# Small routing operations on GpSimd, and weight splits 2 to 4 queued behind the last tiles' routing

## The chip, the cores and the metric

The kernel runs on one core of a Trainium2 chip. The metric is the device time of one launch in microseconds (us). A core has five engines that run side by side, each with its own queue in a fixed order: TensorE (PE in the profile, its weight loads PEld), VectorE (DVE), ScalarE (ACT), GpSimd (POOL) and SyncE (SP), which here only issues transfers.

## The reference, cut to what matters

```python
def reference(q, k, v, moe, moe2):
    # attention: 2 x 8 heads, 576 rows, head size 64; only the 32 largest scores of a row count
    scores = q @ k.T / 8
    kth = np.partition(scores, -32, axis=-1)[..., -32:-31]
    attn = softmax(np.where(scores >= kth, scores, -1e9))
    x = heads_side_by_side(attn @ v)                    # 1152 tokens x 512
    # a gated layer, 512 -> 1536 -> 512
    xn = x / np.sqrt(np.mean(x * x, -1) + 1e-6) * rms_g
    x = (silu(xn @ w_gate) * (xn @ w_val)) @ w_out
    # 8 experts, each token goes to one, at most 288 tokens each, in the tokens' order
    e = np.argmax(x @ router, axis=1)
    for each expert: y = np.maximum(x[its tokens] @ w1[e], 0) @ w2[e]
    return y * softmax(x @ router)[e]                   # 1152 x 512
```

## The kernel before

The 1152 tokens are nine tiles of 128 (`t` = 0 to 8). A tile has four **units** of two heads (`p` = 0 to 35). The function `topk` finds the 32 largest scores of a unit on VectorE: for each head four MAX8 (L324, L336) and three MATCH_REPLACE8 (L333) over 128x576 scores. Beside it run, as generators that are advanced a step at a time:

- `scores` (L310 on TensorE, copy L312 on ScalarE) for the next unit. The score tile `s` has four buffers, so the scores of unit p+1 need the two buffers of unit p-1, which are read last in `weights`, by the subtraction L353 on GpSimd. `weights` itself needs the bias that GpSimd makes of `topk`'s results (L326, L338).
- `values` (L376, L377, L384), `norm` (L389 on), `moe1` (the gated layer: TensorE L450 and L475, GpSimd L465, L466, L470), and `dispatch` (the routing of a tile).
- `convert_all`, in the first 220 us or so: it turns the weights of the gated layer, which come as 64-bit words, into pairs of 16-bit values. `bits` (L157 to L160) and `split` (L219 on) do the large work; `gram` and `scale` (L176 to L217) find a scale for each of the seven weight blocks, in operations on one or four columns.

`dispatch(t)` finds each token's expert and place. On VectorE it has the largest logit (L526), a key (L533), the largest key (L536), a one-hot row `oh` (L539), the expert's first row by a product with `first` and a sum (L547), the token's place by the same with a TensorE result (L550), the overflow test (L553), two additions (L554, L563) and the output scale (L555). TensorE counts with `oh` (L542, L543). GpSimd then writes the tile's 128 rows to their slots in `disp` in memory (L565, the **scatter**). Every token must be scattered before an expert's rows can be read back (`gather`, L772), apart from a first group "a" of 128 rows of expert 0, which is read as soon as tile 7 is scattered; it is issued on ScalarE.

After the attention, expert weights are loaded (L718), measured (`size`: squares L731 on ScalarE, then a chain of one-column operations on VectorE) and split into two 16-bit parts (`convert`: L756 on ScalarE, L758 and L761 on VectorE). Weight 4 is loaded into the buffer that weight 2 leaves, weight 5 into that of weight 3. Then `up` and `down` (L845 to L864) run expert by expert, and `send` (L879 on) writes the result.

A scheduler orders the instructions of each engine when the kernel is built, by priorities (`ahead`, L578) and its own model of durations; what it made is fixed in the program. `tc.issue_after(x)` (L814) makes the instructions of its block on the engine of `x` stand behind `x`. In this kernel it stands over `size(3, 3)` and `convert(3, 3)` with a GpSimd instruction, and neither function has one on GpSimd, so it holds nothing back.

## Time and profile before

| what | value |
|---|---|
| three runs | 708.5, 710.47, 710.53 us; median 710.47 us |
| the profiled execution: its own time | 708.96 us |
| its span, first to last instruction | 707.2 us (1.8 us lie around it) |
| VectorE busy | 627.0 us, 89% of the span |
| TensorE busy | 555.5 us, 79% |
| ScalarE busy | 495.8 us, 70% |
| GpSimd busy | 414.9 us, 59% |

Times inside the program are us from the start of the span. Three parts follow each other: attention with the routing of the first tiles beside it, the gated layer and routing of the last tiles, and the experts. A busy share over the whole span mixes them, so it is read for each part. Instructions of one engine overlap a little at their ends, which a sum of durations counts twice.

### The profile page before, as it was taken

How to read it: one execution, taken by the hardware profiler on the slowest of the kernel's cores; microseconds unless marked ns; L12 is line 12 of the kernel's file. 1: busy time of each engine (PE TensorE's matmuls, PEld its weight loads, DVE VectorE, ACT ScalarE, POOL GpSimd, SP SyncE). 2: the span in 40 equal slices, each digit the busy share in tenths (PEclk: the TensorE clock that was granted, in tenths of full speed). 3: DMA queues.
4: the chain of work that ended last, by engine and by line, in shares of the span. 5: the costliest groups of instructions: out<-in, count | busy, mean ns of one | idle time of the engine just before them, and what ended most of it. 6: DMA issues, size and time to landing. Idle time of an engine off the chain costs nothing.

```text
span 707.2 us, 13015 instructions
## 1 busy us (share of the span) xinstructions
PE 555.5 (79%) x4708; PEld 401.9 (57%) x4708; DVE 627.0 (89%) x1311; ACT 495.8 (70%) x959; POOL 414.9 (59%) x444
## 2 busy tenths in 40 slices
PE   1207424567667999999999999998999489989995
PEld 1106324435344666666656666664645289989994
DVE  3999999999999999999999999999348855999960
ACT  3446537558957879868878797876799537988921
POOL 2786887877696887966767778566631110022312
PEclk9999555679999999999999999999999889999998
DMA  8898171375000001000000000000570449999201
GB/s 244 236 331 282 39 233 38 126 225 188 15 8 8 16 31 43 16 31 10 16 23 16 24 16 24 1 1 16 205 286 1 148 82 382 328 322 347 106 21 38
DMA packets 47016, 80.00 MB, mean 113 GB/s; under 512 B 18732, under 2 KB 23340, under 8 KB 46946
## 3 DMA queue, kind: packets, MB, share of 16 engines
q1 hardware_dynamic: 43954, 74.02, 33.2%
q0 software_dynamic: 1792, 4.83, 1.9%
q8 instruction: 39, 0.64, 0.4%
q10 hardware_dynamic: 1200, 0.26, 0.2%
q14 instruction: 31, 0.25, 0.1%
HBM read 64.35 MB, written 12.27 MB: 108 GB/s over the span
## 4 chain that ended last, share of the span: by engine, by line
DVE 49%; issue 16%; PE 11%; ACT 8%; DMA 8%; POOL 6%; SPq 1%; POOLq 0%; ACTq 0%; DVEq 0%
DVE r L333 14%; DVE m L336 14%; DVE m L324 5%; PE pm L450 4%; DMA wbig<-in_w_out_dram 3%; DVE wbig L157 3%; ACT junk L731 3%; DMA raw<-in_w_dram 3%; POOL out_dram L887 2%; DVE wbig L159 2%; DVE split L761 2%; DVE wbig L228 2%; DMA vt<-in_v_l_dram 2%; PE pm L475 2%; DVE hT L423 1%
## 5 line engine op out<-in xcount | busy, mean ns | idle before, releaser
L450 PE MATMUL pm<-wbig,xn 128*128 128x512 f16 x600 | 152.1, 387 | 8.8 <-POOL wbig L225 3.2
L336 DVE MAX8 m<-r 128x8 f32<-128x576 f32 x216 | 156.8, 745 | 0.3
L845 PEld LDWEIGHTS <-split 128*128 128x128 f16 x1728 | 115.6, 99 | 6.9 <-DMA xbT<-xb 2.5
L310 PE MATMUL tp<-kst,qh 128*128 128x288 f32 (+1 forms) x160 | 65.2, 418 | 63.5 <-ACT s L312 24.2
L353 POOL TENSOR_TENSOR pp<-s,pp 128x576 f32<-128x576 f32 x72 | 102.8, 1442 | 8.6 <-ACT pp L352 8.4
L333 DVE MATCH_REPLACE8 r<-m,r 128x576 f32<-128x576 f32 x144 | 106.3, 740 | 0.0
L450 PEld LDWEIGHTS <-xn 128*128 128x128 f16 x648 | 62.4, 100 | 71.9 <-issue 11.3
L475 PE MATMUL pm<-wbig,hT 128*128 128x512 f16 x324 | 79.1, 383 | 7.7 <-POOL wbig L229 3.7
L310 PEld LDWEIGHTS tp<-kst,qh 128*128 128x128 f32 (+1 forms) x160 | 32.6, 205 | 89.9 <-ACT s L312 32.7
L376 PE MATMUL tp<-ident,pp 128*128 128x128 f32 x324 | 58.7, 298 | 16.1 <-ACT pp L358 7.5
L352 ACT ACTIVATE pp<-s,bias 128x576 f32<-128x576 f32 x72 | 52.0, 773 | 26.4 <-POOL bias L338 26.2
L312 ACT ACTIVATE s<-tp 128x288 f32<-128x288 f32 x144 | 54.8, 412 | 19.2 <-POOL pp L353 15.8
L761 DVE SCALAR_TENSOR_TENSOR split<-raw,sc,split 128x2048 f16<-128x2048 f32 (+1 forms) x32 | 65.8, 2078 | 0.1
L887 POOL DMA_INDIRECT out_dram<-ob,tos x14 | 20.2, 1445 | 73.8 <-ACT ob L885 58.4
L845 PE MATMUL acc<-hE,split 128*128 128x168 f16 (+2 forms) x864 | 58.8, 228 | 3.4 <-ACT junk L731 1.4
L731 ACT ACTIVATE junk<-raw 128x2048 bf16<-128x2048 f32 (+1 forms) x32 | 54.2, 1693 | 9.9 <-DMA raw<-in_w_dram 9.5
L384 PE MATMUL xps<-pt,vt 128*64 128x128 f32 (+1 forms) x800 | 57.8, 284 | 2.9 <-ACT pt L377 2.9
L376 PEld LDWEIGHTS tp<-ident,pp 128*128 128x128 f32 x324 | 42.5, 152 | 31.0 <-ACT pp L358 10.3
L377 ACT ACTIVATE pt<-tp 128x384 f32<-128x384 f32 x108 | 49.3, 494 | 14.9 <-PE tp L376 12.3
L845 PE MATMUL acc<-xgT,split 128*128 128x168 f16 (+1 forms) x768 | 58.0, 239 | 0.0
L358 ACT ACTIVATE pp<-pp,bias 128x576 f32<-128x576 f32 x72 | 56.4, 785 | 0.1
L324 DVE MAX8 m<-s 128x8 f32<-128x576 f32 x72 | 53.6, 745 | 0.0
(198 smaller groups left out, 1233.4 us busy)
## 6 DMA issues: line engine op xcount, KB each, us to landing
raw<-in_w_dram SPq DMA_DIRECT2D x28, 1024.0 KB, 10.2
wbig<-in_w_out_dram SPq DMA_DIRECT2D x6, 1024.0 KB, 8.1
disp<-wraw SPq DMA_DIRECT2D x18, 257.0 KB, 5.5
qraw<-in_q_l_dram SPq DMA_DIRECT2D x72, 64.0 KB, 2.2
wraw<-in_w_gate_dram SPq DMA_DIRECT2D x8, 512.0 KB, 4.5
split<-in_w_dram SPq DMA_DIRECT2D x4, 1024.0 KB, 5.8
kraw<-in_k_l_dram SPq DMA_DIRECT2D x12, 288.0 KB, 4.4
wbig<-in_w_val_dram SPq DMA_DIRECT2D x3, 1024.0 KB, 7.4
```

The source lines that it names most:

```text
L310: nc.tensor.matmul(sp[:c1], x[:, i, :c1], kst[b, hp][:, i, c * HALF:(c + 1) * HALF], start=(n == 0), stop=(n == 1))
L324: nc.vector.max(m[:, i, 0], s[i])
L333: nc.vector.match_replace(r[i], m[:, i, n - 1], src, -3.0e38)
L336: nc.vector.max(m[:, i, n], r[i])
L353: nc.gpsimd.tensor_tensor(w, s[i], w, op=OP.subtract)
L376: nc.tensor.transpose(tp[:, i, :], p2[:, o:o + P], ident)
L384: nc.tensor.matmul(xps[t][rows, hp, c0:c1], v, w, start=(n == 0), stop=(n == 4))
L450: nc.tensor.matmul(a, xn[:, x + c, :], half(i, lo), start=(c == 0 and n == 0), stop=(c == KC - 1 and n == 2))
L475: nc.tensor.matmul(yps, hT[f // KC][:, KC * hi + f % KC, :], half(i, lo), start=(f == 0 and n == 0), stop=(f == NF1 - 1 and n == 2))
L731: nc.scalar.activation(junk, raw[:, g * 2 * BIG // k:(g + 1) * 2 * BIG // k], AF.Square, accum_out=sc[:, 9 + g:10 + g])
L761: nc.vector.scalar_tensor_tensor(lo[:, r], raw[:, r], sc[:, 7:8], hi[:, r], op0=OP.mult, op1=OP.subtract)
L845: nc.tensor.matmul(a, u[:, c, col * P:(col + 1) * P], v[:, c, :a.shape[-1]], start=(c == 0 and n == 0), stop=(c == nk - 1 and n == 2))
```

## The change

It has two halves.

**Operations that move from VectorE to GpSimd.** For tiles 0 to 7: `oh` (L539), the overflow test, the first addition and the output scale (L553 to L555), the slot (L563), and the sum of `norm` (L391). The expert's first row comes from the key `k8` by one multiply-add instead of the product with `first`, and the slot is one operation on pos with two scalars. The last tile keeps these on VectorE. In `gram` and `scale` the one- and four-column operations move too (L189, L198, L203 to L208, L212, L213, L215). Counted in the built program, VectorE has 86 instructions fewer and GpSimd 85 more.

**Where splits and squares stand.** `after(t, ...)` places the work of `convert(2, 2)` behind tile 7's routing (its exponential on ScalarE, its reciprocal on VectorE), that of `convert(3, 3)` behind the last tile's (its exponential on ScalarE, its slot on VectorE), and the squares of weight 4 behind the last tile's exponential on ScalarE.

```diff
-    first = const.tile([P, E], F32, name="first")
-    nc.gpsimd.iota(first, pattern=[[cap, E]], base=0, channel_multiplier=0, allow_small_or_imprecise_dtypes=True)
...
             if b < 6:
-                nc.vector.tensor_tensor(m[:, 0:1], m[:, 0:1], g2[:, 0:1], op=OP.mult)
+                nc.gpsimd.tensor_tensor(m[:, 0:1], m[:, 0:1], g2[:, 0:1], op=OP.mult)
...
         def scale(b, g):
             for _ in g:
                 pass
-            v = nc.vector
+            v = nc.gpsimd
...
-                v.tensor_tensor(tmp[:, 0:1], unit[:, 0:1], unit[:, 1:2], op=OP.min)
-                v.tensor_tensor(tmp[:, 0:1], tmp[:, 0:1], unit[:, 2:3], op=OP.min)
+                nc.vector.tensor_tensor(tmp[:, 0:1], unit[:, 0:1], unit[:, 1:2], op=OP.min)
+                nc.vector.tensor_tensor(tmp[:, 0:1], tmp[:, 0:1], unit[:, 2:3], op=OP.min)
...
-        nc.vector.tensor_scalar(rs, sums[t], EPSD, None, op0=OP.add)
+        (nc.gpsimd if t < NT - 1 else nc.vector).tensor_scalar(rs, sums[t], EPSD, None, op0=OP.add)
...
-    scat = []
+    scat, behind = [], {}
+
+    @contextmanager
+    def after(t, *engines):
+
+        with ExitStack() as stack:
+            for e in engines:
+                stack.enter_context(tc.issue_after(behind[t, e].ins))
+            yield
...
-        nc.scalar.activation(ex, lg, AF.Exp, bias=nm[:, 0:1], accum_out=nm[:, 1:2])
+        behind[t, "act"] = nc.scalar.activation(ex, lg, AF.Exp, bias=nm[:, 0:1], accum_out=nm[:, 1:2])
...
-        nc.vector.tensor_scalar(oh, rank8, k8[:, 0:1], None, op0=OP.is_equal)
+        (nc.vector if t == NT - 1 else nc.gpsimd).tensor_scalar(oh, rank8, k8[:, 0:1], None, op0=OP.is_equal)
...
-        nc.vector.scalar_tensor_tensor(scr[:, 0], first, 1.0, oh, op0=OP.mult, op1=OP.mult, accum_out=pos[:, 1:2])
+        ev = nc.vector if t == NT - 1 else nc.gpsimd
+        ev.tensor_scalar(pos[:, 1:2], k8[:, 0:1], -float(cap), float(cap * E), op0=OP.mult, op1=OP.add)
...
-        nc.vector.reciprocal(nm[:, 3:4], nm[:, 2:3])
+        behind[t, "dve"] = nc.vector.reciprocal(nm[:, 3:4], nm[:, 2:3])
...
-        nc.vector.tensor_scalar(pos[:, 2:3], pos[:, 0:1], float(cap), NOWHERE, op0=OP.is_ge, op1=OP.mult)
-        nc.vector.tensor_tensor(pos[:, 3:4], pos[:, 0:1], pos[:, 1:2], op=OP.add)
-        nc.vector.tensor_scalar(yd[:, DM:DM + 1], nm[:, 3:4], yn[:, 2:3], 1.0 / YS, op0=OP.mult, op1=OP.mult)
+        ev.tensor_scalar(pos[:, 2:3], pos[:, 0:1], float(cap), NOWHERE, op0=OP.is_ge, op1=OP.mult)
+        ev.tensor_tensor(pos[:, 3:4], pos[:, 0:1], pos[:, 1:2], op=OP.add)
+        ev.tensor_scalar(yd[:, DM:DM + 1], nm[:, 3:4], yn[:, 2:3], 1.0 / YS, op0=OP.mult, op1=OP.mult)
...
-        nc.vector.tensor_tensor(slot, pos[:, 3:4], pos[:, 2:3], op=OP.add)
+        x = ev.tensor_scalar(slot, pos[:, 0:1], pos[:, 1:2], pos[:, 2:3], op0=OP.add, op1=OP.add)
+        if t == NT - 1:
+            behind[t, "dve"] = x
...
     convert(1, 1)
-    convert(2, 2)
+    with after(NT - 2, "act", "dve"):
+        convert(2, 2)
     fetch_w()
-    with tc.issue_after(scat[-1].ins):
-        size(3, 3)
+    size(3, 3)
+    with after(NT - 1, "act", "dve"):
         convert(3, 3)
...
         if n == 4:
-            size(ORDER[4], 4)
+            with after(NT - 1, "act"):
+                size(ORDER[4], 4)
```

The built order of the changed kernel has its own line numbers. Up to L66 of the kernel before they are the same; from L70 to `scat` (L484) a line stands two earlier; behind it, six to eleven later.

On GpSimd, the routing of tile 2 up to its scatter. Before (L564 is the count, L565 the scatter, L465, L466 and L470 the gated layer, L326 and L338 the biases of `topk`, L353 the subtraction of `weights`):

```order
L564 TENSOR_TENSOR cum<-cum,oh 128x8
L291 TENSOR_TENSOR ql<-qraw,qh 128x256
L326 TENSOR_SCALAR bias<-m 128x2
L465 TENSOR_TENSOR th<-th,gs 128x512
L466 TENSOR_TENSOR th<-th,gs 128x512
L404 TENSOR_TENSOR x<-x,rs 128x512
L338 TENSOR_SCALAR bias<-m 128x2
L565 DMA disp<-yd,slot 2320x514
L470 TENSOR_TENSOR gs<-th,gs 128x512
L409 TENSOR_SCALAR ss<-ss 128x1
L353 TENSOR_TENSOR pp<-s,pp 128x576 x2
```

And in the change, the same tile (L351 is the subtraction, L573 the count; the scatter follows the last row):

```order
L545 TENSOR_SCALAR oh<-rank_72,k_3050 128x8
L554 TENSOR_SCALAR pos<-k_3050 128x1
L351 TENSOR_TENSOR pp<-s,pp 128x576
L324 TENSOR_SCALAR bias<-m 128x2
L351 TENSOR_TENSOR pp<-s,pp 128x576
L562 TENSOR_SCALAR yd<-nm,yn 128x1
L463 TENSOR_TENSOR th<-th,gs 128x512
L573 TENSOR_TENSOR cum<-cum,oh 128x8
L560 TENSOR_SCALAR pos<-pos 128x1
L561 TENSOR_TENSOR pos<-pos 128x1
L464 TENSOR_TENSOR th<-th,gs 128x512
L570 TENSOR_SCALAR slot<-pos 128x1
```

Six operations (L545, L554, L562, L560, L561, L570) now stand in the same queue as the subtractions and the biases; they stood on VectorE.

On ScalarE, the last tile's routing. Before (L481 takes the gated layer's result, L492 is the first operation of the last tile's routing, L531 its exponential, L731 the squares of weight 4, L772 and L785 the reading of group "a"):

```order
L756 ACTIVATE split_5637<-raw_5639,sc 128x1024 x2
L481 ACTIVATE yx<-pm,st 128x512
L731 ACTIVATE junk,sc<-raw_5638 128x2048
L492 ACTIVATE xu<-px 128x512
L772 DMA_TRANSPOSE xgT<-disp 128x8x128
L785 DMA notes_5889<-disp 128x2
L497 ACTIVATE yd,yn<-yx 128x512
L731 ACTIVATE junk,sc<-raw_5638 128x2048
L518 ACTIVATE yd<-yx,yn 128x512
L531 ACTIVATE ex,nm<-lg,nm 128x8
```

In the change (L479, L498, L537, L740, L781 and L794 are the same operations; L765 splits weight 2 in the first row and weight 3 in the tenth):

```order
L765 ACTIVATE split_5634<-raw_5636,sc 128x1024 x2
L420 ACTIVATE hT<-pm 128x512
L479 ACTIVATE yx<-pm,st 128x512
L781 DMA_TRANSPOSE xgT<-disp 128x8x128
L794 DMA notes_5887<-disp 128x2
L498 ACTIVATE xu<-px 128x512
L503 ACTIVATE yd,yn<-yx 128x512
L524 ACTIVATE yd<-yx,yn 128x512
L537 ACTIVATE ex,nm<-lg,nm 128x8
L765 ACTIVATE split_5635<-raw_5637,sc 128x1024 x2
L740 ACTIVATE junk,sc<-raw_5636 128x2048
```

The squares of weight 4 went behind the exponential, and the reading of group "a" went ahead of the last tile's first operation.

On VectorE, the end of tile 7's routing in the change (L558 is its reciprocal, L557 its place, L767 and L770 the split of weight 2, L421 the low half of the last tile's third hidden group, which TensorE waits for):

```order
L558 RECIPROCAL nm<-nm 128x1
L140 TENSOR_SCALAR sc<-sc 128x1
L767 TENSOR_SCALAR split_5634<-raw_5636,sc 128x1024 x2
L746 TENSOR_SCALAR sc<-st 128x1
L770 SCALAR_TENSOR_TENSOR split_5634<-raw_5636,sc,split_5634 128x1024 x2
L557 SCALAR_TENSOR_TENSOR scr,pos<-px,oh 128x8
L770 SCALAR_TENSOR_TENSOR split_5634<-raw_5636,sc,split_5634 128x1024
L748 TENSOR_SCALAR sc<-sc 128x1
L770 SCALAR_TENSOR_TENSOR split_5634<-raw_5636,sc,split_5634 128x1024
L421 TENSOR_TENSOR hT<-pm,hT 128x512
```

In the kernel before, the same four L761 stood among tile 7's earlier steps (its key, its largest key and its one-hot row), and the split of weight 3 came between tile 7's last addition and the last tile's routing.

## Rows read from the trace of the kernel before

**Rows 1.** Stretches: length, busy us (count) of PE, PEld, DVE, ACT, POOL; clock, DMA.
```profile
20.00:240.00 220.00, 121.42 (x764) 83.27 (x765) 219.84 (x412) 141.13 (x289) 172.54 (x157) 0.83 0.44 137
240.00:497.00 257.00, 247.94 (x1773) 161.58 (x1771) 256.19 (x594) 205.35 (x466) 186.07 (x221) 1.00 0.06 18
497.00:558.00 61.00, 56.16 (x334) 30.27 (x332) 37.24 (x100) 49.04 (x90) 22.48 (x26) 1.00 0.44 161
...
574.00:707.00 133.00, 116.78 (x1720) 114.59 (x1717) 97.19 (x159) 85.97 (x95) 23.30 (x17) 0.98 0.69 214
```
**Rows 2.** VectorE groups, 20 to 240 us: count | busy us, mean ns | idle before.
```profile
L198 DVE TENSOR_SCALAR st<-gk,st 128x4 f32<-128x4 f32 x6 | 5.6, 928 | 0.0
L189 DVE TENSOR_TENSOR m<-m,st 128x1 f32<-128x1 f32 x6 | 1.9, 320 | 0.0
L208 DVE TENSOR_TENSOR st<-st 128x1 f32<-128x1 f32 x3 | 1.9, 635 | 0.0
L391 DVE TENSOR_SCALAR rs<-sums 128x8 f32<-128x8 f32 x3 | 1.5, 486 | 0.0
L205 DVE TENSOR_TENSOR st<-st 128x1 f32<-128x1 f32 x3 | 1.3, 420 | 0.0
```
**Rows 3.** VectorE groups, 240 to 485 us, the same columns.
```profile
L563 DVE TENSOR_TENSOR slot<-pos 128x1 int32<-128x1 f32 x6 | 4.1, 676 | 0.0
L547 DVE SCALAR_TENSOR_TENSOR scr<-first,oh 128x8 f32<-128x8 f32 x6 | 4.0, 665 | 0.0
L554 DVE TENSOR_TENSOR pos<-pos 128x1 f32<-128x1 f32 x6 | 3.4, 564 | 0.0
...
L539 DVE TENSOR_SCALAR oh<-rank,k 128x8 bf16<-128x8 f32 x6 | 2.2, 373 | 0.0
L391 DVE TENSOR_SCALAR rs<-sums 128x8 f32<-128x8 f32 x5 | 1.7, 345 | 0.0
```
**Rows 4.** GpSimd groups of the whole span, the same columns.
```profile
L409 POOL TENSOR_SCALAR ss<-ss 128x1 f32<-128x1 f32 x9 | 1.9, 212 | 2.6 <-ACT xu L407 2.5
L564 POOL TENSOR_TENSOR cum<-cum,oh 128x8 bf16<-128x8 bf16 x9 | 1.8, 202 | 8.3 <-PE px L543 8.2
```
**Rows 5.** Who waited for whom: us in total, times, longest us.
```profile
ACT pp L352 <- POOL bias L338: 26.2, 20, 4.1
...
ACT s L312 <- POOL pp L353: 15.8, 9, 4.4
```
**Rows 6.** Timeline at the end of tile 2's routing: start us, us, engine, instruction, [idle before].
```profile
353.06 1.10 POOL L565 DMA_INDIRECT disp<-yd,slot  x1 [0.28 <-issue]
...
353.87 1.40 DVE L336 MAX8 m<-r 128x8 f32<-128x576 f32 x2
...
355.57 2.77 POOL L353 TENSOR_TENSOR pp<-s,pp 128x576 f32<-128x576 f32 x2
...
357.02 0.71 ACT L312 ACTIVATE s<-tp 128x288 f32<-128x288 f32 x2 [2.45 <-POOL pp L353]
...
357.97 0.74 DVE L324 MAX8 m<-s 128x8 f32<-128x576 f32 x1
```
**Rows 7.** Timeline of a unit with no scatter ahead of it.
```profile
467.82 1.01 ACT L312 ACTIVATE s<-tp 128x288 f32<-128x288 f32 x3
...
471.83 0.75 DVE L324 MAX8 m<-s 128x8 f32<-128x576 f32 x1
```
**Rows 8.** Timeline of the routing of tiles 7 and 8.
```profile
558.30 1.43 POOL L565 DMA_INDIRECT disp<-yd,slot  x1 [2.92 <-DVE sc L746]
...
561.85 1.91 ACT L731 ACTIVATE junk<-raw 128x2048 bf16<-128x2048 f32 x1 [3.25 <-DMA raw<-in_w_dram]
562.56 1.36 ACTq L772 DMA_TRANSPOSE xgT<-disp  x1
...
564.39 1.88 PE L503 MATMUL px<-rg,xu 128*128 128x8 f32 x8 [5.08 <-ACT xu L492]
...
571.17 1.06 POOL L565 DMA_INDIRECT disp<-yd,slot  x1 [1.19 <-DVE slot L563]
```

2 lines of the change are left out of this document (1 added, 1 removed).

## Prediction

> **What bounds the kernel now.** I read the busy time by stretch first [rows 1]. From 20 to 497 us VectorE is busy for 219.84 of 220 us and 256.19 of 257 us: it never waits, so in this part the time is the sum of what VectorE issues, and an operation taken off it is worth its own length, as long as VectorE then still finds its inputs ready. GpSimd is at 78% (172.54 of 220) and then 72% (186.07 of 257). From 497 to 558 us VectorE is down to 37.24 of 61 us and TensorE is at 56.16: the gated layer of the last tiles sets the pace. From 574 us on TensorE is busy for 116.78 of 133 us, so the expert part starts when the last scatter lets it, and its length is its own.
>
> Then the groups of VectorE's small operations in those stretches [rows 2, 3]. The reader should look at the mean against the width: one column should cost little, and yet L198 takes 928 ns, L563 676 and L547 665. VectorE records no idle time before them, and neighbours of the same width take a third of it or less (L189 320 ns, L391 345): I read the excess as a wait inside the operation, at a time when GpSimd is busy three quarters of the time.
>
> Third, what VectorE waits for next once its own work shrinks. A unit's scores need the buffers that the subtraction L353 frees, so there is a loop over two units: end of `topk`, bias L338, L352, L353, TensorE, copy L312, `topk` two units later. The waits show it: ScalarE stood before L352 for 26.2 us until the bias came, and before L312 for 15.8 us until L353 was done [rows 5]. Behind tile 2's scatter (1.10 us on GpSimd) L353 runs from 355.57, L312 waits 2.45 us for it and ends at 357.73, and `topk` starts at 357.97: a margin of 0.24 us [rows 6]. In a unit without a scatter ahead the copies end at 468.83 and `topk` starts at 471.83: 3.0 us [rows 7]. So the loop is close behind VectorE, and it runs through GpSimd, where the change puts work.
>
> **The moved operations, 20 to 240 us.** Two MAX8 in a row take 1.40 us [rows 6], one 0.745, so an operation holds VectorE for about 0.08 us less than its recorded length. Off VectorE come L198, 6 x 0.85 = 5.1 us; L208, 3 x 0.555 = 1.7; L189, 6 x 0.24 = 1.4; L391, 3 x 0.41 = 1.2; L205, 3 x 0.34 = 1.0 [rows 2]. That is 10.4 us; the remaining one-column operations of `scale` I leave out as too small. Bounds: all 10.4, or 0 where the results now come late from GpSimd's queue, since `scale` feeds `split`, whose casts stand on VectorE in a fixed order. GpSimd has 47 us free in this stretch and gets some 30 operations of 0.2 us [rows 4], 6 us. I take 6.5, nearer to the upper end, because VectorE's large work here leaves the loop above more room than later.
>
> **The moved operations, 240 to 485 us.** This is the routing of tiles 0 to 5. L563, 6 x 0.596 = 3.6 us; L547, 6 x 0.585 = 3.5; L554, 6 x 0.484 = 2.9; L539, 6 x 0.293 = 1.8; L391, 5 x 0.265 = 1.3 [rows 3]. Sum 13.1 us, 2.2 per tile; L553 and L555 are left out. What of it can be kept depends on the loop. A tile's four units hold two of its rounds. The two margins above average 1.6 us, so 3.2 us for a tile. Against that, GpSimd gets eight operations per tile at about 0.21 us [rows 4], 1.7 us, of which perhaps half, 0.85, stand between a `topk` and its subtraction. That leaves 2.35 us of room for 2.2 us of gain: on average just enough, but margins run from 0.24 to 3.0 us and room unused in one place doesn't help another. I take a little over half: 7.5 us. Bounds: 0, where the loop is full, and 13.1. The multiply-add that replaces L547, and the slot made of two scalars, are among the eight.
>
> New waits. VectorE's L550 needs the TensorE count, which now needs `oh` from GpSimd; for tile 2 the built order has six operations of `topk` and one L423 between the largest key and L550, at about 0.66 us each [rows 6] some 4.5 us, in which a GpSimd operation behind one subtraction (2.77 us for two [rows 6]) and TensorE's count fit. I cost it at nothing; without that cover it would be up to 1.4 us a tile. The reciprocal of `norm` waits for a sum that GpSimd does units earlier: nothing.
>
> **From 497 us to the last scatter.** Before, the last tile's first ScalarE operation stood behind the squares of weight 4, which waited 3.25 us for their data and ran 1.91 us; TensorE idled 5.08 us until L503 at 564.39 [rows 8]. The change takes the squares away from there, and by that alone up to 5.08 us. But the built order puts the reading of group "a" ahead of that operation, and it needs tile 7's scatter in memory: it was issued at 562.56, 4.3 us behind that scatter's start at 558.30 [rows 8]. Tile 7's scatter comes earlier only by as much as its routing does, and four of its steps are now on GpSimd beside the two-input splits of weight 2 on VectorE. The 4.3 us and the 1.36 us of issue stay. I put that scatter some 2 us earlier and the net gain at 1.5 us; bounds 0 and 5. The low half of the last tile's hidden group still stands behind four L770, so the end of the gated layer I leave where it was. The split of weight 3, now behind the last slot, runs beside group "a" and is needed only by expert 1's second product: nothing, and if that cover failed, its VectorE operations would hold the low half of group "a".
>
> **Sum.** 6.5 + 7.5 + 1.5 = 15.5 us off the profiled execution's 708.96 is 693.5 us. The median of the three runs is 1.5 us above that execution, so I forecast **695.0 us**.
>
> **A rule that speaks against the change.** On GpSimd a two-input operation on 8 columns took 202 ns (L564) and a one-input one 212 ns (L409) [rows 4], where VectorE's one-column L554 took 564 [rows 3]. The Trainium skill, GPSIMD Engine Reference, section 4.1 (Engine selection), says that elementwise work belongs on VectorE, two-input operations being about twice as slow on GpSimd. The trace here has it the other way for such small tiles. By that rule, set on VectorE's lengths here, the moved operations would take 4.4 us of GpSimd per tile, and the third rival below would come to about 727 us instead of 713.
>
> **Rivals.**
>
> *Everything is kept.* For: VectorE has no idle time at all. Against: the margin of 0.24 us. 10.4 + 13.1 + 5 = 28.5 off: 680.5, as a median 682 us.
>
> *The loop takes over.* GpSimd's queue frees the score buffers no earlier than now, so the steady gain is lost: 5 early, 1.5 in steady running, 1 at the end, 701.5, as a median 703 us. For: the 15.8 us of waits for L353 are there already [rows 5]. Against: margins of 3 us away from the scatters.
>
> *Slower.* The eight operations stand inside the loop, at a place where it has no room, before L353: each tile's loop then grows by their 1.7 us, or with hand-over time 2.0, and VectorE's gain there is nothing. 6 x 2.0 = 12 lost against 6.5 and 1.5 gained is 4 us more: 713, as a median 714.5 us. It decides from 8 / 6 = 1.35 us per tile. For: L338 and L353 share the queue with them, and a wait for L338 has been 4.1 us long [rows 5]. Against: they are spread over more than one unit, and GpSimd is idle for a quarter of the time [rows 1].
>
> *No effect.* TensorE, at 247.94 of 257 us by the profile [rows 1], sets the pace, and the tail only swaps one wait for another: 708 to 712 us. Against: the profile models the ends of matmuls, and VectorE had no wait for it.
>
> **How the numbers follow.** Forecast (687 to 701 us) 0.57, all kept 0.10, loop 0.20, slower 0.08, no effect 0.05. About 0.3%, 2.1 us, can be told from no change. Faster: 0.57 + 0.10 + 0.20 = 0.87; within 0.3%: 0.05; slower: 0.08. The range, 684 to 707 us, reaches into the case of all kept and beyond that of the loop; outside are the slower case, that of no effect and part of that of all kept, together 0.2.
>
> **What would show it.** VectorE's last MAX8 should come about 14 us earlier and its busy share before it fall a little below 100%, with short waits before L324 that ScalarE's copy ends. If those waits add up to 10 us or more, the loop rival is right; if there are none, everything was kept. The moved groups should read 0.2 to 0.4 us each on GpSimd. In the tail the last L503 should start on the release of the reading of group "a", no longer behind L731, and the distance from the last MAX8 to the last scatter should shrink by 1 to 2 us. I am wrong if VectorE stands before L550 or its casts waiting for GpSimd, if the distance from the last MAX8 to the end grows, or if GpSimd's small operations take over 0.5 us.

## The result, and the profile after

The changed kernel is slower, by 0.7%. Over 19 runs each, taken in turn, its median is 715.49 us (712.67 to 717.7) against 710.01 us (706.53 to 713.64): a ratio of 1.0074 with a 95% interval of 1.0057 to 1.0091. The forecast was 695.0 us, with a range up to 707.

The profiled executions have spans of 713.2 us after and 707.2 us before, so they show the same 6 us. Cutting both spans at the same four events, all times in us from the span's start, says where they come from:

| event | before | after | difference |
|---|---|---|---|
| VectorE's last MAX8 ends (attention) | 497.1 | 482.9 | 14.2 earlier |
| the last tile's gated layer ends on TensorE | 557.8 | 554.9 | 2.9 earlier |
| last scatter issued | 571.2 | 569.3 | 1.9 earlier |
| end of the span | 707.2 | 713.2 | 6.0 later |

So VectorE gained the 14 us that were forecast, 11.3 of them were gone by the end of the gated layer, and the expert part, which was left out of the sum, grew by 7.9 us. The page of the changed kernel begins:

```profile
span 713.2 us, 12997 instructions
PE 560.2 (79%) x4708; PEld 404.2 (57%) x4708; DVE 612.0 (86%) x1216; ACT 496.9 (70%) x959; POOL 448.4 (63%) x529
```

Busy time by stretch of the changed kernel, with the columns of [rows 1]:

```profile
20.00:240.00 220.00, 124.41 (x783) 84.38 (x784) 218.58 (x388) 143.69 (x294) 181.70 (x194) 0.81 0.44 138
240.00:497.00 257.00, 251.13 (x1801) 163.28 (x1800) 241.88 (x542) 208.78 (x472) 201.36 (x264) 1.00 0.09 29
497.00:558.00 61.00, 52.28 (x290) 27.32 (x288) 34.60 (x79) 41.93 (x74) 25.78 (x32) 0.96 0.37 135
574.00:713.00 139.00, 120.81 (x1720) 118.63 (x1719) 99.19 (x162) 85.42 (x94) 28.02 (x17) 0.94 0.66 205
```

In the second row VectorE, 256.19 of 257 us in [rows 1], is down to 241.88, and TensorE, 247.94 there, is now at 251.13. The first engine was relieved and the second had 9 us to give. The granted clock of the last row is 0.94, a mean of time at 2.4 GHz (1.00) and at 1.2; it was 0.98.

GpSimd's groups that answer to [rows 2, 3], from 20 to 485 us (count | busy us, mean ns | idle before):

```profile
L570 POOL TENSOR_SCALAR slot<-pos 128x1 int32<-128x1 f32 x6 | 2.3, 382 | 0.0
L545 POOL TENSOR_SCALAR oh<-rank,k 128x8 bf16<-128x8 f32 x6 | 1.9, 316 | 0.1
L196 POOL TENSOR_SCALAR st<-gk,st 128x4 f32<-128x4 f32 x6 | 1.6, 273 | 0.5 <-DVE st L137 0.5
L561 POOL TENSOR_TENSOR pos<-pos 128x1 f32<-128x1 f32 x6 | 1.2, 193 | 0.5
```

And what VectorE waited for from 240 to 485 us (us in total, times, longest us):

```profile
DVE m L322 <- ACT s L310: 1.9, 4, 0.8
```

L322 is the first MAX8 (L324 before) and L310 the copy of the scores: the loop over two units cost 1.9 us.

### The profile page after: what moved, and what is told of

It is laid out like the page before. It is cut to its first block, busy times and chain, and to the rows that moved or that the text cites. A ratio compares the mean times of both kernels' runs of the same rounds, so it can differ in the third digit from the quotient of the medians.

```text
span 713.2 us, 12997 instructions
## 1 busy us (share of the span) xinstructions
PE 560.2 (79%) x4708; PEld 404.2 (57%) x4708; DVE 612.0 (86%) x1216; ACT 496.9 (70%) x959; POOL 448.4 (63%) x529
## 4 chain that ended last, share of the span: by engine, by line
DVE 34%; PE 25%; issue 13%; POOL 12%; DMA 8%; ACT 6%; SPq 2%; ACTq 0%; POOLq 0%; DVEq 0%
PE pm L448 8%; DVE r L331 8%; DVE m L334 7%; PE pm L473 5%; DMA raw<-in_w_dram 5%; DVE wbig L155 4%; DVE wbig L157 3%; PE xps L382 3%; POOL pp L351 3%; DVE m L322 3%; DVE wbig L226 2%; PE tp L374 2%; PE tp L308 2%; POOL out_dram L897 2%; DVE split L770 2%
## 5 line engine op out<-in xcount | busy, mean ns | idle before, releaser
L448 PE MATMUL pm<-wbig,xn 128*128 128x512 f16 x600 | 154.5, 391 | 7.5 <-ACT xn L420 3.5
L855 PEld LDWEIGHTS <-split 128*128 128x128 f16 x1728 | 118.5, 100 | 10.3 <-issue 6.0
L308 PE MATMUL tp<-kst,qh 128*128 128x288 f32 (+1 forms) x160 | 63.7, 411 | 65.0 <-ACT s L310 22.5
L351 POOL TENSOR_TENSOR pp<-s,pp 128x576 f32<-128x576 f32 x72 | 102.7, 1438 | 11.5 <-ACT pp L350 11.0
L310 ACT ACTIVATE s<-tp 128x288 f32<-128x288 f32 x144 | 54.4, 411 | 24.9 <-POOL pp L351 20.6
L897 POOL DMA_INDIRECT out_dram<-ob,tos x14 | 23.8, 1703 | 72.2 <-ACT ob L895 70.1
L855 PE MATMUL acc<-hE,split 128*128 128x168 f16 (+2 forms) x864 | 60.9, 233 | 8.7 <-DVE hE L866 6.4
L770 DVE SCALAR_TENSOR_TENSOR split<-raw,sc,split 128x2048 f16<-128x2048 f32 (+1 forms) x32 | 65.7, 2077 | 0.0
L374 PE MATMUL tp<-ident,pp 128*128 128x128 f32 x324 | 56.6, 294 | 10.9 <-ACT pp L356 10.3
L740 ACT ACTIVATE junk<-raw 128x2048 bf16<-128x2048 f32 (+1 forms) x32 | 54.2, 1694 | 10.2 <-DMA raw<-in_w_dram 9.8
L374 PEld LDWEIGHTS tp<-ident,pp 128*128 128x128 f32 x324 | 41.0, 149 | 26.2 <-ACT pp L356 14.3
L322 DVE MAX8 m<-s 128x8 f32<-128x576 f32 x72 | 53.7, 746 | 2.0 <-ACT s L310 1.9
```

The costliest lines, as they stand in the source:

```text
L308: nc.tensor.matmul(sp[:c1], x[:, i, :c1], kst[b, hp][:, i, c * HALF:(c + 1) * HALF], start=(n == 0), stop=(n == 1))
L322: nc.vector.max(m[:, i, 0], s[i])
L351: nc.gpsimd.tensor_tensor(w, s[i], w, op=OP.subtract)
L374: nc.tensor.transpose(tp[:, i, :], p2[:, o:o + P], ident)
L448: nc.tensor.matmul(a, xn[:, x + c, :], half(i, lo), start=(c == 0 and n == 0), stop=(c == KC - 1 and n == 2))
L770: nc.vector.scalar_tensor_tensor(lo[:, r], raw[:, r], sc[:, 7:8], hi[:, r], op0=OP.mult, op1=OP.subtract)
```

## The experiments

Seventeen kernels ran. Two theories stood at the start. *Placement*: the moves to GpSimd gain, and what the second half of the change places loses more. *Cover*: the moves' gain is small in itself, since TensorE bounds the stretch behind the last MAX8. They do not exclude each other, so each needed a price. In the table a ratio is against executions of the kernel before that were taken beside the run's own (their medians lie between 709.5 and 710.9 us), with its 95% interval; the five other columns are the profiled execution's events as above, all in us, and all of TensorE's idle time behind the last scatter.

| run | median us | ratio | MAX8 | gated layer | scatter | idle | span |
|---|---|---|---|---|---|---|---|
| before | 710.01 | 1 | 497.1 | 557.8 | 571.2 | 7.9 | 707.2 |
| after | 715.49 | 1.0074 [1.0057, 1.0091] | 482.9 | 554.9 | 569.3 | 13.0 | 713.2 |
| 1: moves alone | 707.22 | 0.9954 [0.9941, 0.9967] | 480.4 | 553.1 | 567.2 | 8.4 | 704.2 |
| 2: placements alone | 721.56 | 1.0158 [1.0134, 1.0183] | 496.7 | 559.6 | 575.5 | 15.2 | 720.3 |
| 3: split of weight 3 free | 707.48 | 0.9962 [0.9945, 0.9979] | 481.2 | 553.8 | 569.1 | 7.8 | 704.6 |
| 4: squares of weight 4 free | 715.67 | 1.006 [1.0039, 1.008] | 480.3 | 551.4 | 567.4 | 13.3 | 711.8 |
| 5: before, gated layer cut | 711.06 | 1.0018 [0.9999, 1.0036] | 494.6 | 562.0 | 572.4 | 6.5 | 708.9 |
| 6: moves, gated layer cut | 702.78 | 0.9904 [0.9872, 0.9936] | 483.7 | 545.6 | 562.5 | 11.5 | 699.7 |
| 7: split of 3 behind group "a" | 705.51 | 0.9934 [0.9912, 0.9957] | 479.5 | 552.0 | 566.9 | 8.4 | 703.5 |
| 8: last tile first | 711.61 | 1.001 [0.9989, 1.003] | 481.1 | 553.8 | 563.0 | 10.4 | 707.9 |
| 9: squares of weight 5 later | 717.6 | 1.0128 [1.0102, 1.0153] | 479.8 | 553.0 | 566.8 | 14.9 | 714.5 |
| 10: 8 with reading on SyncE | 706.62 | 0.9965 [0.9942, 0.9988] | 481.1 | 553.9 | 569.7 | 9.9 | 706.8 |
| 11: 10 and 7 | 706.41 | 0.9959 [0.9936, 0.9981] | 479.9 | 552.7 | 566.8 | 9.0 | 703.3 |
| 12: moves of the scales | 705.04 | 0.9922 [0.9892, 0.9952] | 488.2 | 552.2 | 564.3 | 7.5 | 702.6 |
| 13: moves of the routing | 719.99 | 1.0137 [1.0107, 1.0167] | 481.3 | 558.9 | 577.0 | 15.0 | 716.2 |
| 14: 10, "a" behind the count | 710.5 | 1.0004 [0.9983, 1.0026] | 481.0 | 554.0 | 560.9 | 13.6 | 707.8 |
| 15: 14 and 7 | 712.66 | 1.0036 [1.0012, 1.0059] | 479.2 | 550.7 | 558.5 | 14.0 | 707.9 |
| 16: 12, squares of 4 placed | 704.05 | 0.9907 [0.9872, 0.9942] | 491.0 | 554.4 | 566.4 | 8.0 | 703.8 |
| 17: 16 and 7 | 714.94 | 1.0063 [1.004, 1.0086] | 492.1 | 556.6 | 567.8 | 13.8 | 715.4 |

### The two halves apart (1 and 2)

Run 1 is the changed kernel without its three placements:

```diff
-    with after(NT - 2, "act", "dve"):
-        convert(2, 2)
+    convert(2, 2)
...
-    with after(NT - 1, "act", "dve"):
-        convert(3, 3)
+    convert(3, 3)
...
-            with after(NT - 1, "act"):
-                size(ORDER[4], 4)
+            size(ORDER[4], 4)
```

> The changed kernel with its three placements taken back (split of weight 2, split of weight 3 and squares of weight 4 stand where they stood before); the operations stay on GpSimd. Theory A, the placements lose the time: the expert part, from the last scatter to the end, goes back from 143.9 us to about 136, and 3 to 6 us of VectorE's 12 us gain are left, so some 704 to 707 us against 710. Theory B, the moves to GpSimd lose it (tiles' gated layer falls behind, the throttle takes more): no better than the changed kernel, 714 to 716 us, with the expert part still over 141 us.

Run 2 is the kernel before with those three placements (the opposite edit) and the `behind` entries that they need.

> The kernel before with the three placements alone, no operation moved to GpSimd. Theory A: the expert part grows to 143 or 144 us from the last scatter, and tile 7's routing, now on VectorE, puts that scatter no earlier than 569: 715 to 719 us. Theory B: the placements are worth their 1 to 2 us in front of the last scatter and cost nothing behind it: 707 to 709 us.

The moves alone gain, 0.9954, and the placements alone lose, 1.0158. So the loss is in the placements; and of the 16.7 us by which run 1's last MAX8 comes earlier, 3.0 are left at the end of its span, which is the second question.

### Which placement loses (3, 4 and 7)

Run 3 frees one placement of the changed kernel, the split of weight 3; run 4 frees another, the squares of weight 4.

```diff
-    with after(NT - 1, "act", "dve"):
-        convert(3, 3)
+    convert(3, 3)
```

> The changed kernel with the split of weight 3 alone set free from the last tile's routing. Theory A, in the form that this split holds the low half of group a (it ended at 574.45 instead of 571.90) and pushes everything behind it: half or more of the 8 us come back, 708 to 711 us, and the wait of TensorE ahead of the first product down of group a is under 2 us. If the loss comes from another placement or from the moves: 714 to 716 us.

```diff
-            with after(NT - 1, "act"):
-                size(ORDER[4], 4)
+            size(ORDER[4], 4)
```

> The changed kernel with the squares of weight 4 alone set free from the last tile's exponential. If their late place delays the weights 4 to 7 and with them the second half of the expert part: 4 or 5 us come back, 710 to 712 us, while the last scatter comes some 2 us later again. If the split of weight 3 is the cause: 714 to 717 us.

The split of weight 3 alone carries the loss: without its placement the ratio is 0.9962, as good as run 1, and with it and without that of the squares 1.006, as bad as the change. Run 1 and run 3 differ by the other two placements and agree, and run 4 agrees with the change, so neither of those two does anything that can be measured here.

The mechanism stands in VectorE's timeline of the changed kernel (start us, us, engine, instruction, [idle before]):

```profile
562.78 0.15 DVE L516 TENSOR_SCALAR yn<-yn 128x1 f32<-128x1 f32 x1 [10.55 <-ACT yd L503]
...
568.16 0.26 DVE L570 TENSOR_SCALAR slot<-pos 128x1 int32<-128x1 f32 x1
568.35 1.41 DVE L767 TENSOR_SCALAR split<-raw,sc 128x1024 f16<-128x1024 f32 x2
569.67 4.86 DVE L770 SCALAR_TENSOR_TENSOR split<-raw,sc,split 128x1024 f16<-128x1024 f32 x4
574.45 0.68 DVE L866 SCALAR_TENSOR_TENSOR hE<-acc,hE 128x512 f16<-128x512 f32 x1
```

The same stretch of run 3:

```profile
550.30 1.41 DVE L767 TENSOR_SCALAR split<-raw,sc 128x1024 f16<-128x1024 f32 x2
...
551.70 4.87 DVE L770 SCALAR_TENSOR_TENSOR split<-raw,sc,split 128x1024 f16<-128x1024 f32 x4
561.16 0.15 DVE L516 TENSOR_SCALAR yn<-yn 128x1 f32<-128x1 f32 x1 [4.59 <-ACT yd L503]
```

Free, the split fills a hole that VectorE has anyway. Behind the last slot it leaves the hole empty (10.55 us) and takes 6.1 us ahead of L866, the low half of group "a", the first thing TensorE needs once the last scatter is out. TensorE in the changed kernel:

```profile
575.19 1.44 PE L855 MATMUL acc<-hE,split 128*128 128x128 f16 x12 [4.39 <-DVE hE L866]
576.52 6.54 PE L855 MATMUL acc<-hE,split 128*128 128x128 f16 x83
```

And in run 3:

```profile
571.52 4.79 PE L854 MATMUL acc<-hE,split 128*128 128x128 f16 x83 [0.64 <-DVE sc L748]
```

The wait is 4.39 us, and the same 83 matmuls then take 6.54 us instead of 4.79. Runs 2, 4 and 9, which have the same placement, show a wait at this place too, of 4.78, 3.93 and 4.40 us. The granted clock of the stretch from 570 to 590 us, after and in run 3 (columns of [rows 1]):

```profile
570.00:590.00 20.00, 14.28 (x247) 13.90 (x245) 13.24 (x19) 6.51 (x7) 3.24 (x2) 0.83 0.82 216
```
```profile
570.00:590.00 20.00, 15.88 (x282) 15.52 (x280) 9.33 (x16) 7.17 (x8) 3.04 (x3) 0.91 0.84 230
```

Behind the wait of 4.39 us, from 575 to 583 us, the granted clock is 0.67, a mean of the two levels. Later waits are longer as well. TensorE's waits from 560 to 612 us, after:

```profile
PE px L509 <- ACT xu L498: 5.4, 1, 5.4
PE acc L855 <- DVE hE L866: 4.6, 2, 4.4
PE st L745 <- DVE s L743: 3.6, 1, 3.6
PE acc L855 <- DVE sc L748: 1.8, 1, 1.8
```

Before:

```profile
PE px L503 <- ACT xu L492: 5.1, 1, 5.1
PE acc L845 <- DMA xbT<-xb: 2.3, 1, 2.3
PE st L736 <- DVE s L734: 1.3, 1, 1.3
```

L743, L745 and L748 are steps of `size`. The 3.6 us are not a wait for the split itself: VectorE, ahead of L743, had been idle for 6.66 us until ScalarE's squares of weight 5 (L740) were done. VectorE and TensorE of the changed kernel:

```profile
592.24 0.17 DVE L743 CAST s<-sc 128x2 bf16<-128x2 f32 x1 [6.66 <-ACT junk L740]
```
```profile
586.13 2.70 PE L855 MATMUL acc<-xgT,split 128*128 128x168 f16 x35
592.46 0.19 PE L745 MATMUL st<-s,ones 128*128 128x1 bf16 x2 [3.63 <-DVE s L743]
```

And TensorE in run 3:

```profile
590.93 1.02 PE L854 MATMUL acc<-hE,split 128*128 128x48 f16 x34
591.79 0.19 PE L745 MATMUL st<-s,ones 128*128 128x1 bf16 x2
```

L743 runs at 591.12 us in run 3 and at 593.11 in run 7 below, where L745 waits 0.58 us for it. So L743 is at most 1.1 us later here than where TensorE has no such wait; what differs is TensorE's built order. Here 35 matmuls of expert 1's first product stand ahead of L745 and 61 behind it; in run 3 all 96 stand ahead, and 34 more. The placement thus costs in two ways, by the low half that it holds and by the order that the scheduler built around it. Runs 3 and 7 take both back, so the two are not priced apart.

From the last scatter to the end, after and in run 3 (columns of [rows 1]):

```profile
569.29:713.20 143.91, 122.32 (x1747) 120.02 (x1744) 103.89 (x166) 88.63 (x100) 30.57 (x18) 0.94 0.64 200
```
```profile
569.10:704.60 135.50, 119.08 (x1737) 116.83 (x1734) 97.53 (x160) 86.67 (x97) 27.41 (x18) 0.97 0.68 212
```

TensorE is busy 3.2 us longer, at a lower granted clock, and idle 5.2 us longer (13.0 against 7.8): together the 8.4 us by which this part is longer than in run 3.

Run 7 keeps the split late, but puts it behind that low half:

```diff
-    with after(NT - 1, "act", "dve"):
-        convert(3, 3)
...
-            nc.vector.scalar_tensor_tensor(hl, a, 0.0, hh, op0=OP.max, op1=OP.subtract)
+            behind[k] = nc.vector.scalar_tensor_tensor(hl, a, 0.0, hh, op0=OP.max, op1=OP.subtract)
...
     up("a", 0, WA)
+    with tc.issue_after(behind["a"].ins):
+        convert(3, 3)
```

> The changed kernel with the split of weight 3 one step later still: behind the low half of group a's hidden values instead of behind the last slot. If the split costs by holding that low half (TensorE waits 4.4 us there and its clock falls): that wait goes, TensorE's first product down of group a runs some 4 us earlier, and about half of the loss comes back, 709 to 712 us; the rest stays because the split of weight 4 is then queued behind it and ahead of the result of that product. If the lateness of weight 3 itself, or of the buffer it frees, is what costs: 715 to 720 us.

```profile
569.12 0.68 DVE L864 SCALAR_TENSOR_TENSOR hE<-acc,hE 128x512 f16<-128x512 f32 x1
569.72 1.41 DVE L767 TENSOR_SCALAR split<-raw,sc 128x1024 f16<-128x1024 f32 x2
```
```profile
569.85 4.79 PE L853 MATMUL acc<-hE,split 128*128 128x128 f16 x83 [0.65 <-DVE hE L864]
```

VectorE above, TensorE below: the low half is done first, the wait is 0.65 us and the matmuls take 4.79 us again. I had expected part of the loss to stay, for the hole is empty here too (VectorE's idle time ahead of L516 is 10.92 us); all of it came back. So in this kernel the loss is the place ahead of the low half, with the order that it brings, and not the unused hole. That run 7 is better than run 3 is not shown: their intervals overlap.

### Why 14 us of VectorE were worth so little (5 and 6)

If TensorE has a backlog behind the last MAX8, then taking work off TensorE must do nothing in the kernel before and something in run 1. Both runs leave out one of the three passes of the gated layer's products (the one on the low parts of the activations) for tiles 0 to 5; run 5 is otherwise the kernel before, run 6 is run 1.

```diff
...
-            for n, (hi, lo) in enumerate(((0, 0), (0, 1), (1, 0))):
+            ps = ((0, 0), (0, 1), (1, 0))[:2 if t < 6 else 3]
+            for n, (hi, lo) in enumerate(ps):
...
```

(the second product of the layer; the edit of the first is alike)

> The kernel before without a third of the gated layer's matmuls in tiles 0 to 5 (the pass of the low parts of the activations is left out there, 36 of 108 matmuls of 512 columns a tile; tiles 6 to 8 are whole). 10 of them take 2.33 us at full clock, so about 50 us of TensorE's work is gone. Theory T, that VectorE sets the pace before and TensorE after the moves: here little comes back, the last MAX8 stays near 497 us and the time at 704 to 710 us. If TensorE already sets the pace before the change: under 700 us.

> The same matmuls left out of the kernel with the moves to GpSimd alone (707.2 us whole). Theory T, the 16 us by which the last MAX8 comes earlier are lost to a gated layer that cannot follow: with its work cut, most of them reach the end, so this run is 9 to 15 us below the run before it, where the pair without the cut differs by 3.7 us; the last tile's gated layer ends 9 us or more earlier than in the run before it, where it was 4.8. Rival: the gain is lost elsewhere (loads of the expert weights, routing, expert part), then the pair differs by 2 to 5 us as without the cut.

The cut changes nothing in the kernel before (1.0018, its interval takes in 1). Under the moves it brings the end of the gated layer from 553.1 (run 1) to 545.6 us and the time to 0.9904. The moves are worth 8.3 us between runs 5 and 6, where they are worth 3.7 between the kernel before and run 1. The size was missed, 9 to 15 us having been expected. The sign is as expected, but the pair is not clean. From the last MAX8 to the end of the gated layer the granted clock is 0.91 in run 5 and 0.97 in run 6 (1.00 before), and that end comes 16.4 us earlier in run 6 where the last MAX8 comes 10.9 earlier. So part of the 8.3 us is not TensorE's backlog.

The backlog can be read without the cut. From the last MAX8 to the end of the gated layer, before, then after:

```profile
497.14:557.84 60.70, 56.02 (x333) 30.20 (x331) 36.94 (x99) 48.74 (x88) 22.34 (x26) 1.00 0.44 161
```
```profile
482.91:554.91 72.00, 65.26 (x376) 34.81 (x373) 36.63 (x85) 50.56 (x93) 33.34 (x40) 0.99 0.37 138
```

When VectorE is done with the attention, TensorE still has 65.3 us of work up to the end of the gated layer, where it had 56.0: 376 matmuls instead of 333. These 9.2 us are most of the 11.3 that were gone by that end; the other 2.1 are idle time (6.7 us against 4.7). From 480 to 500 us, before, then run 1:

```profile
480.00:500.00 20.00, 17.07 (x118) 10.22 (x116) 17.10 (x35) 13.05 (x27) 12.22 (x16) 1.00 0.04 14
```
```profile
480.00:500.00 20.00, 20.00 (x138) 12.09 (x136) 2.52 (x8) 12.09 (x25) 9.08 (x10) 1.00 0.64 231
```

VectorE has nothing to do there any more (2.52 us), and TensorE has no gap (20.00).

### Which moves are worth something (12 and 13)

Run 12 takes only the moves of `gram` and `scale`, run 13 only those of routing and `norm`, both from the kernel before and without placements. In both the first row comes from the key and the slot is one operation, on VectorE in run 12.

```diff
...
-            v = nc.vector
+            v = nc.gpsimd
...
```

> Of the moves, only the small operations of the weights' scales stand on GpSimd; routing and norm stay on VectorE, and no placement is made. By the prediction's terms VectorE saves 6.5 us of this up to 240 us; by the trace of the changed kernel its units start 4.3 us earlier at 222 us. If VectorE still sets the pace behind that: last MAX8 near 492 us and 2 to 4 us off the end, 706 to 708 us. If TensorE's backlog takes it: 708.5 to 711 us.

```diff
-        (nc.vector if t == NT - 1 else nc.gpsimd).tensor_scalar(oh, rank8, k8[:, 0:1], None, op0=OP.is_equal)
...
-        ev = nc.vector if t == NT - 1 else nc.gpsimd
+        nc.vector.tensor_scalar(oh, rank8, k8[:, 0:1], None, op0=OP.is_equal)
...
+        ev = nc.vector
...
```

(run 13 as the minus lines, run 12 as the plus lines)

> Of the moves, only the routing of tiles 0 to 7 and the sum of the norm stand on GpSimd; the scales stay on VectorE, no placement. By the prediction's term VectorE saves 7.5 us, last MAX8 near 487 us. Theory T (TensorE's backlog behind the last MAX8 sets the end once VectorE is some 4 us faster): no more than 4 us reach the end, 706 to 709 us, and the two halves together (707.2) bring hardly more than the better of them. Additive rival: the two halves' gains add up to the 3.5 us of both.

The rewritten first row and slot save VectorE time by themselves: before, they took 4.0 and 4.1 us of it (L547, L563 in [rows 3]), in run 12 0.8 and 1.5 (L554, L570, 20 to 485 us). So what run 12 gains is not the scales' alone.

Run 12 saves 8.9 us of VectorE up to the last MAX8 (488.2) and run 1 16.7 (480.4), yet the gated layer ends at 552.2 and 553.1 us. TensorE is without a gap in both:

```profile
480.00:500.00 20.00, 20.00 (x136) 12.00 (x133) 12.13 (x37) 15.36 (x33) 14.40 (x16) 1.00 0.30 108
```

That is run 12's row. So the routing's moves, 7.8 us on VectorE on top of those of run 12, bring nothing at the end of the gated layer. Run 12 alone, at 0.9922, is better than the whole change.

Run 13 is a miss: VectorE was relieved by 15.8 us and the kernel is slower than before. (The two halves do not add up: 8.9 and 15.8 us alone, 16.7 together.) Its built order has the squares of weight 4 ahead of the last tile's copy of the gated result on ScalarE:

```profile
557.69 1.91 ACT L740 ACTIVATE junk<-raw 128x2048 bf16<-128x2048 f32 x1 [2.92 <-DMA raw<-in_w_dram]
560.54 1.91 ACT L740 ACTIVATE junk<-raw 128x2048 bf16<-128x2048 f32 x1 [0.84 <-ACT junk L740]
562.45 0.67 ACT L479 ACTIVATE yx<-pm,st 128x512 f32<-128x512 f32 x1
```

L479 could have run at 558.9, when TensorE had its input ready. The last scatter went out at 577.0 us, 5.8 later than before. A run of one half of an edit is therefore not the edit less the other half: the scheduler sorts the tail anew each time.

### Is the last scatter what the end waits for (8, 10, 11, 14 and 15)

Run 8 is run 1 with the squares of weight 4 placed as in the change, and the last tile's path cleared: the reading of group "a" stands behind the last tile's ScalarE work, its row has a buffer of its own, tile 7's routing is back on VectorE.

```diff
...
-        yd = mx.tile([P, ROW], F32, name="yd")
+        yd = mx.tile([P, ROW], F32, name="x" if t == NT - 1 else "yd")
...
-            gather("a", 0, 0, WA, ew, nc.scalar)
-            notes("a", 0, 0, WA, ew, nc.scalar)
+            with tc.issue_after(behind[t, "act"].ins), tc.issue_after(yh8.ins):
+                gather("a", 0, 0, WA, ew, nc.scalar)
+                notes("a", 0, 0, WA, ew, nc.scalar)
...
```

> The moves to GpSimd and the squares of weight 4 behind the last exponential, splits 2 and 3 free; new: the reading of group a stands on ScalarE behind the last tile's exponential and scaled copy instead of ahead of its first operation, the last tile has a row buffer of its own, and tile 7's routing stays on VectorE. TensorE waits 4.7 us ahead of the last router product for ScalarE, which stands behind that reading (it waits for tile 7's scatter to land). If that wait is on the path: the last scatter comes 3 to 5 us earlier and the time is 702 to 704 us. If the scatter's landing or group a's reading is what ends last anyway: 706 to 708 us.

The last scatter came at 563.0 us, 4.1 earlier than in run 1, and the time is 1.001. VectorE of run 8:

```profile
566.66 0.69 DVE L868 SCALAR_TENSOR_TENSOR hE<-acc,hE 128x512 f16<-128x512 f32 x1 [1.71 <-ACT hE L867]
...
571.51 0.14 DVE L884 CAST to<-xb 48x1 int32<-48x1 f32 x1 [4.15 <-DMA xb<-disp,rest]
...
572.27 0.68 DVE L868 SCALAR_TENSOR_TENSOR hE<-acc,hE 128x512 f16<-128x512 f32 x1
```

A cast that waits 4.15 us for the gathered rows of group "b" stands between the two halves of group "a". Run 10 mends this: the reading goes on SyncE ahead of the load of weight 4, the casts behind the low half, `up("b")` behind the products of `down("a")`.

```diff
...
-            with tc.issue_after(behind[t, "act"].ins), tc.issue_after(yh8.ins):
-                gather("a", 0, 0, WA, ew, nc.scalar)
-                notes("a", 0, 0, WA, ew, nc.scalar)
+            gather("a", 0, 0, WA, ew, nc.sync)
+            behind["notes"] = notes("a", 0, 0, WA, ew, nc.sync)
...
-    fetch_w()
+    with tc.issue_after(behind["notes"].ins):
+        fetch_w()
...
-    up("b", 0, WB)
+    with tc.issue_after(behind["down", "a"].ins):
+        up("b", 0, WB)
...
```

> As the run on the last tile, but the reading of group a is issued by SyncE, ahead of the load of weight 4, so that ScalarE's queue holds no wait for tile 7's scatter and that scatter lands without the load beside it (it took 7 us with it and 4.3 us in the kernel before without); and two orders are fixed: the casts of the row numbers stand behind the low half of group a on VectorE, group b's first product behind group a's second on TensorE. If what undid the earlier last scatter was those two in-order holds: 700 to 704 us, last scatter before 563, group a's low half held for nothing. If the earlier scatter cannot be used at all: 706 to 710 us.

Run 11 is run 10 with the split of weight 3 behind the low half of group "a", by run 7's edit.

> The run before this one with the split of weight 3 behind the low half of group a, so that VectorE is free for the last tile's routing as soon as its inputs are there. If the split in front of the routing costs anything there (VectorE took the first routing operation right at the split's end): 1 us better than the run before. If behind group a it delays the split of weight 4 and group a's result: 1 to 2 us worse.

Both gain what run 1 gains (0.9965 and 0.9959). In run 10 the last scatter was at 569.7 us, not the expected 563 or less: 21 matmuls of group "a" stood on TensorE ahead of the last tile's logits and waited 3.07 us for their rows. Run 14 puts group "a" behind the last count; run 15 adds run 7's edit.

```diff
...
-    up("a", 0, WA)
+    with tc.issue_after(behind["count"].ins):
+        up("a", 0, WA)
```

> As the run with the last tile's reading on SyncE (706.6 us), and group a's first product stands behind the last tile's count on TensorE. There 21 of its matmuls stood ahead of the last router product and waited 3.1 us for group a's rows, and 53 in all ahead of the count. If this is what kept the last scatter at 569.7: it comes at 560 to 563, and the time falls to 699 to 703 us. If group a's own chain (its reading, two products at the low clock) sets the start of the expert part: 705 to 708 us, with the scatter early and unused.

> The run before this one, with the split of weight 3 behind the low half of group a as well. If VectorE's queue in front of the last routing matters: the last scatter 1 to 2 us earlier still and 0 to 2 us off the end. If the split delays group a's result and the split of weight 4 there: 1 to 3 us slower than the run before.

The scatter came at 560.9 and 558.5 us, the earliest of all, and the times are 1.0004 and 1.0036. From the last scatter to the end these kernels take 146.8 and 149.3 us, where before takes 136.0. So an early last scatter is not enough: what it gave was taken back behind it. In run 14 TensorE is idle for 13.6 us there against 8.4 in run 1, and it has more left to do, 1797 matmuls (124.7 us) against 1753 (120.1), since group "a" now stands behind the last count.

### Two more placements (9, 16 and 17)

Run 9 is the changed kernel with the squares of weight 5 behind group "b"'s high half on ScalarE, to remove the 3.6 us wait for L743.

```diff
...
-        if n + 1 < 2 * E:
+        if n == 5:
+            with tc.issue_after(behind["act", "b"].ins):
+                size(ORDER[5], 5)
+        if 5 < n + 1 < 2 * E:
```

> The changed kernel, split of weight 3 left where the change puts it; only the squares and the scale of weight 5 move, behind the hidden values of group b on ScalarE and into the next step of the list of weights. In the changed kernel they stand ahead of those hidden values, and TensorE waits 3.6 us for them within expert 1. If the loss has two parts, the low half of group a held by the split (4.4 us of wait and a slower clock) and this second wait: 3 to 5 us come back, 710 to 713 us. If the first part alone sets the end: 714 to 717 us.

A miss: that wait is gone, but others stand later (one of 4.17 us from 668 us on), and the time is 1.0128. Waits in the weights' chain that are removed in one place come back in another.

Run 16 is run 12 with the placement of the squares of weight 4; run 17 adds run 7's edit.

```diff
-            size(ORDER[4], 4)
+            with after(NT - 1, "act"):
+                size(ORDER[4], 4)
```

> Only the scales' small operations on GpSimd, and of the placements only that of weight 4's squares; splits 2 and 3 free. In the run with the scales alone those squares, waiting 1.9 us for their data, stood ahead of the last tile's first ScalarE operation, and TensorE waited 3.3 us. If that wait is on the path: the last scatter comes 1 to 2 us earlier and the time is 703 to 705 us. If the weights' chain (load, squares, split) sets the expert part: 705 to 707 us.

> The run before this one with the split of weight 3 behind the low half of group a. With the moves of routing it was worth 0 to 2 us (705.5 against 707.5). If what it gives is a free VectorE in front of the last routing, the same here: 702 to 704 us. If it only shifts the split of weight 4 to later: 705 to 708 us.

Run 16 is the fastest kernel that does all the work, 704.05 us (0.9907), ahead of both the kernel before and the changed one; with those of runs 12 and 7 its interval overlaps. In run 17 the place of the split that cured the change in run 7 costs: 1.0063. Up to 600 us TensorE's order is much as in run 16, then it waits for VectorE, for 1.75 us up to 610.2 us (a split, L770) and for 3.0 us up to 620.5 (by the profile L743). ScalarE shows what is late: its built order has hidden values that wait for TensorE (5.18 and 2.02 us) ahead of the next squares, which start at 600.2 us; in run 16 they start at 587.5, and the loads behind them at 601.8 us instead of 607.9.

## Why the prediction was wrong

The sum was 15.5 us of gain, and the profiled execution lost 6.0: a miss of 21.5 us. Of these 11.3 were lost up to the end of the gated layer and 7.9 in the expert part; behind that end and up to the last scatter 1.5 were to be gained and 1.0 was lost; and 0.2 more than forecast had come at the last MAX8. By the steps:

- **The moved operations on VectorE: right as a sum.** 6.5 + 7.5 = 14.0 us were forecast, and the last MAX8 came 14.2 us earlier. That the two terms add up to it is luck. Units that began at 226.31 and 245.41 us before begin at 222.01 and 243.29: 2 to 4 us had come by then, where 6.5 were forecast, and 10 to 12 came behind, where 7.5 were. The groups of moved operations take 185 to 438 ns on GpSimd, near the forecast (they are seven per tile, not eight); VectorE's waits for the loop's copy are 1.9 us, so the rival of the loop is out, and so is that of GpSimd in the loop. The reading of the long one-column operations as waits is borne out: L554 and L563, 564 and 676 ns in [rows 3], take 0.15 us each in the last tile of the kernel before. So VectorE is not the slower engine for them by itself, where the prediction took the trace to have it that way. Part of the wait moved on: the key, which stayed on VectorE, takes 879 ns in tiles 0 to 5 instead of 490. The 4.4 us per tile in the rule against the change double L539 and L391 too, which read one tile each, 0.5 us of the 2.2.
- **"an operation taken off it is worth its own length": the step that failed.** It holds up to the last MAX8. Behind it TensorE sets the pace, with a backlog that its share in [rows 1] (247.94 of 257) already allowed. Of 14.2 us 2.9 were left at the end of the gated layer, and TensorE's work from the last MAX8 to that end grew from 56.0 to 65.3 us. Runs 5 and 6 agree in sign: less TensorE work does nothing without the moves and brings 7.5 us with them. The rival of no effect named this very engine and number, with a chance of 0.05; its counter-argument, that VectorE had no wait for TensorE, only says which engine bounds now, not how far the next one is behind.
- **The split of weight 3, "nothing": wrong by some 8 us.** Its working looked at when the result is needed (expert 1's second product) and not at what stands behind it on VectorE. The sentence that it would hold the low half of group "a" if the cover failed described what happened (a wait of 4.39 us), but gave it no price; run 3 against the changed kernel prices it at 0.9962 against 1.0074, about 8 us. This is the step that turned the sign.
- **The squares of weight 4 and the split of weight 2.** By the squares up to 5.08 us were in reach and 1.5 net were taken. Freeing the squares (run 4) or both (run 1 against run 3) makes no measurable difference.
- **The tail.** The start of L509, the last tile's logits, on the reading of group "a" came as forecast: L509 waited 5.4 us, where L503 waited 5.08 [rows 8]. Tile 7's scatter was issued 6.6 us earlier (551.70 against 558.30), not 2, but took 7.8 us to land instead of 4.2, so that the last one gained 1.9. The distance from the last MAX8 to the last scatter was to shrink by 1 to 2 us; it grew from 74.0 to 86.4, the backlog again.
- **The signs of error that were named.** The distance from the last MAX8 to the end did grow, from 210.1 to 230.3 us. GpSimd's small operations took over 0.5 us only in tile 7's routing (1.14 to 1.21 us, below).
- **The rival "Slower".** Its 714.5 us lies within 1 us of the measured 715.49, by luck: it has VectorE's steady gain lost to the loop, and that gain came.

What stays open: the part from the last scatter to the end takes either 135 to 139 us or 144 to 149 us in these kernels. In runs 8, 14 and 15 a part of the difference is work of group "a" that comes behind an earlier scatter. For the others, which order of the later weights' squares, scales and splits decides between the two was not settled; run 17 shows that one and the same edit can fall on either side, there by the order on ScalarE.

## What to carry to other kernels

Before an operation taken off a full engine is credited with its length, read the next engine's share in the same stretch and up to the next stage: 248 of 257 us means that at most some 9 us come through, and here 2.9 did. When a wide operation is placed behind X on an in-order engine, ask two things beside when its result is needed: what stands next in that queue, and who waits for it. And where a scheduler builds the order, compare the whole built order behind each edit, for it moves more than the edit names (run 13).
